# A routed layer of experts on one NeuronCore: the list of next experts placed behind the third slot's gathered tokens, and three closing branches nested

## Chip, core and metric

One core of a Trainium2 chip runs the whole program in one launch. The metric is the device time of one execution in microseconds (us), the median of several runs. The program's instructions lie on five engines, each with its own queue, which wait for one another by semaphores: TensorE (PE; PEld is its weight load), VectorE (DVE), ScalarE (ACT), GpSimd (POOL) and SyncE (SP, here the issuer of plain loads). DMA engines move data between HBM and the on-chip memory; gathers and scatters by a list of indices are issued by GpSimd, large loads by SP.

## The reference

The program computes three stages on 1536 tokens of 512 numbers: a windowed attention with block summaries, a dense layer with ELU, and a layer of 8 experts in which each token goes to one expert. Only the last one matters here:

```python
logits = x @ w_gate
e_idx = np.argmax(logits, axis=1)
probs = softmax(logits)
gate_w = probs[np.arange(N), e_idx]
eom = 1.0 / (1.0 + np.exp(-(x @ w_output_gate)))
for e in range(E):
    mask = e_idx == e
    h = np.maximum(x[mask] @ w1[e], 0.0)
    ye = h @ w2[e]
    out[mask] = gate_w[mask, None] * eom[mask, e, None] * ye
```

An expert's weights are w1 (512x1024) and w2 (1024x512), in float32.

## The kernel before, in words

`part1` computes attention and the dense layer; its last steps already choose two experts from the first 1152 tokens and load the weights of the first of them. `part2` calls `second`, which is the layer of experts, and ends with three branches for rare loads of tokens.

The tokens are sorted into *slots* of 128 that share an expert. Slots 0 and 1 are the early ones; slots 2 to 10 are full slots, the entries 11 and 12 of `SEQ` are pairs of half slots of 64 tokens with an expert each, and entries 13 to 15 are the three conditional ones (`PX`). The order is 0, 1, 2, 3, 4, 11, 5, 6, 12, 7, 8, 9, 10. "The third slot" is number 2. For each slot:

- `x_load` (key `xg`, L1082): GpSimd gathers 128 rows of 2 KB from `mdram`; the gather of the slot two places on is issued behind the transposes of this one.
- `x_T` (key `xT`, L1096): TensorE transposes them in four matmuls into one PSUM bank (`T`, a single one); `x_hi2` (`xh`, L1101, ScalarE) and `x_lo2` (`xl`, L1105, VectorE) write them as a high and a low float32r half, and with the low half the bank is free for the next slot's transposes.
- `mm1` (L1121) and `mm2` (L1164): 24 matmuls each (high by high, low by high, high by low weights). The half slots use plain float32 weights (`mm1_two` L1130, `mm2_two` L1173).
- `evac2` (L1177, ScalarE) scales the result, and `scatter` (L1180, GpSimd) writes it to the output by a list of row numbers.

The weights of the full slots have one place on the chip, `w2s`, with a high and a low half for each of 16 blocks of 128x512 floats, and a raw copy in `wo`. `renew(slot, part)` (key `cv`, branch at L1204, conversions L1189 and L1195) is a branch on ScalarE and VectorE: only where the slot's expert differs from the one before does it convert the raw blocks of this part (8, 4 and 4 blocks). Behind each part `load_next` (key `ld`, L1402 to L1411) makes SP load the blocks of the *next different* expert into `wo`, on the condition that it isn't the one loaded before. Which expert that is stands in `nxi`, the list of next experts; `route_a3` (key `a3`, L948 to L964, eight instructions of VectorE) computes it. `route_a5` (key `a5`, L985 to L1000, eight instructions) computes the experts of the half slots and the number that decides the three closing branches. The half slots' weights come by `w_direct` (L1054): 256 KB a load, 25 of them at once into memory that is free by then (`spare`), the rest as places come free; they are issued behind a5.

The order of all this is written by a small planner in `second`. Each operation is entered with a key, an engine, an estimated duration and the keys it must stand behind (`op(key, engine, duration, deps, function)`); the planner picks, over and over, the operation that can start first by its estimates, and emits it. So `deps` set the place of an instruction in its engine's queue; the waits that the data need are set by the framework from the tiles that are read and written. In the order that results before the change, VectorE does a3 and a5 right behind the lists of tokens (`li`), SP issues the three loads of `ld` 1 and then the 25 direct loads, and the transposes of the fifth slot (`xT` 4) stand on TensorE behind the last matmul of slot 1 and ahead of the first matmul of slot 2.

At the end, each of the three `If` blocks holds the loads, the gather and the whole work of one pair of half slots; with these inputs none is taken. An engine that skips a block still passes a compare-and-branch and instructions that bring the semaphores to where the block would have left them; on GpSimd one of them is INC_SWDGE_SEM (L1425).

Of the kernel before, what the change touches and what calls it, by code (L numbers as in the profile page):

```python
# [67 lines left out]
KF = 11  # L68
PB, PX = 2, 3
# [10 lines left out]
class Prog:  # L80
# [1132 lines left out]
    def second(self, seq, t, start=False):  # L1213

        nc, N, C = self.nc, len(seq), COST
# [9 lines left out]
        def mm(q, key, d, deps, fn, used=()):  # L1225
            pe[q].append((key, d, deps, fn, used))

        def op(key, eng, d, deps, fn):
            fixed.append((key, eng, d, deps, fn))
# [41 lines left out]
        f = [i for i in range(N) if full[i]]  # L1271
        for p, i in zip(f, f[1:]):
            known = [("f", 2)] if i > 1 else []
            op(("cv", i, 0), "Act", C["if"], [("on", "m1", p, 1, 3) if i in (1, 3) else ("gl", p, 1), ("xl", i)] + known, lambda i=i: self.renew(seq[i], 0))
            op(("cv", i, 1), "Act", C["if"], [("on", "m2", p, 3), ("cv", i, 0)] + known, lambda i=i: self.renew(seq[i], 1))
            op(("cv", i, 2), "Act", C["if"], [("on", "m2", p, 7), ("cv", i, 1)] + ([("o", p)] if i > 1 else []) + known, lambda i=i: self.renew(seq[i], 2))
            for part in range(3):
                if seq[i] not in nxt:
                    continue
                op(("ld", i, part), "SP", 0.1, [("cv", i, part), ("a3",)], lambda i=i, part=part: self.load_next(nxt[seq[i]], PARTS[part]))  # L1280

        half, at = [], {}
        if start:
            J = NBLK - 1
            for i in range(TPB[J]):
                e, d = ("DVE", C["l"]) if i == 1 else ("Act", C["a"])
                mm("c", ("yl", i), C["m"], [], lambda i=i: self.mm_y1(J, NF - 1, i))
                op(("m", i), e, d, [("yl", i)], lambda i=i: self.out_y1(J, i))
                op(("md", i), "Pool", C["g"], [("m", i)], lambda i=i: self.store_m(nc.gpsimd, J, i))
            for i in range(TPB[J]):  # L1290
                e, d = ("DVE", C["l"]) if i == 1 else ("Act", C["a"])
                mm("c", ("lt", i), C["t"], [("m", i)], lambda i=i: self.lg_turn(J, i))
                op(("mt", i), e, d, [("lt", i)], lambda i=i: self.lg_parts(J, i))
            for i in range(TPB[J]):
                mm("c", ("lg", i), 0.84, [("mt", i)], lambda i=i: self.lg2(J, i))
            op(("lv",), "DVE", 0.12, [("lg", i) for i in range(TPB[J])], self.lg3)
            op(("rb",), "DVE", 1.62, [("lv",)], lambda: self.route_block(J))
            mm("c", ("cnt",), 0.05, [("rb",)], self.count)
            mm("c", ("rm",), 0.05, [("rb",)], lambda: self.rank_mm(TE, NTT, self.fin))
            op(("left",), "DVE", 0.1, [("cnt",)], self.left)  # L1300
            op(("ga",), "DVE", 0.3, [("rb",)], lambda: self.route_gate_a(J))
            op(("ge",), "Act", 0.25, [("ga",)], lambda: self.route_gate_e(J))
            op(("a2",), "DVE", 2.75, [("left",)], self.route_a2)
            op(("rk",), "DVE", 0.35, [("rm",)], lambda: self.rank_of(TE, NTT, self.fin))
            op(("gb",), "DVE", 0.6, [("ge",)], lambda: self.route_gate_b(J))
            op(("gc",), "Pool", 1.4, [("gb",)], lambda: self.route_gate_c(J))
            op(("a4",), "DVE", 1.05, [("a2",)], self.route_a4)
            op(("b1",), "DVE", 2.3, [("a4",), ("rk",)], self.route_b)
            op(("pp",), "Pool", 0.58 * (NTT - PD), [("b1",)], lambda: self.places(nc.gpsimd, PD, NTT))
            op(("pv",), "DVE", 0.2 * PD, [("b1",)], lambda: self.places(nc.vector, 0, PD))  # L1310
            op(("b2",), "DVE", 1.45, [("b1",), ("gc",)], self.route_w)
            mm("c", ("inv",), 0.4, [("b2",), ("pp",), ("pv",)], lambda: self.invert(self.slots_of(), NTT))
            op(("li",), "DVE", 1.4, [("inv",)], lambda: setattr(self, "L_", self.lists("L", self.slots_of(), NL)))
            for i in (2, 3):
                op(("xg", i), "Pool", C["g"], [("li",)], lambda i=i: self.x_load(seq[i]))
            op(("f", 2), "Act", 0.46, [("li",)], lambda: self.flag(2))
            op(("a3",), "DVE", 1.6, [("li",)], self.route_a3)
            op(("a5",), "DVE", 1.75, [("li",)], self.route_a5)
            for i in range(2):
                done["xl", i] = 0.0  # L1320

            for i in range(16):
                if i < WN:
                    done["w", chain[0], i] = 0.0
                    continue
                self.ew[0, i] = self.new_place(f"wi{i}")
                op(("h0", i), "Act", C["hAct"], [], lambda i=i: self.conv_hi("Act", 0, i, self.ew[0, i]))
                op(("w", 0, i), "DVE", C["l"], [("h0", i)], lambda i=i: self.last_w(i))
        else:
            done["xg", 0] = C["xg"]  # L1330
            for i in range(16):
                done["w", chain[0], i] = C["xg"]
            half = [(0.0, p) for i in range(8) for p in self.float_places(f"wi{i}")]
# [15 lines left out]
        while any(pe.values()) or fixed:  # L1349
# [20 lines left out]
            st, _, d, kind, o, eng = best  # L1370
            t[eng] = end = st + d
            if kind == "pe":
                q, o = o
# [39 lines left out]
    def part2(self):  # L1413
        nc, tc = self.nc, self.tc
        J = NBLK - 1
        self.split_g(J, NF - 1)
        self.mm_y(J, NF - 2)
        for k, s in enumerate(range(KF + PB + PX)):
            self.par[s] = k % 2
        self.flag(0)  # L1420
        self.flag(1)
        self.second((0, 1) + SEQ, START2, True)
        n = nc.values_load(self.esi[0:1, LF + NY:], min_val=0, max_val=4 * NL, skip_runtime_bounds_check_because="a sum of counts of slots")  # L1423
        for s in range(KF + PB, KF + PB + PX):
            with tc.If(n > 2 * (s - 2)):  # L1425
                w = self.sets(s)[0]
                for i in range(16):
                    self.w_direct(w, i, self.rw[i])
                self.x_load(s)
                self.second((s,), dict(PE=0, Act=0, DVE=0, Pool=0))  # L1430
# [63 lines left out]
```

## Time and profile before

| | us |
|---|---|
| median of three runs | 575.3 |
| lowest and highest of them | 572.5, 576.26 |
| the profiled execution | 575.26 |
| its span, first to last instruction | 573.1 |
| TensorE's mean granted clock, share of full speed | 0.968 |

Times in the profile count from the start of the span. A row of a timeline has the start, the duration, the engine, the line, the operation, what it writes and reads, how often, and in brackets the idle time before it with what ended it. Engines with a q (DVEq, POOLq, SPq) are their queues: branches, semaphores, DMA issues. PEclk is the granted clock of TensorE, 1.00 for 2.4 GHz and 0.50 for 1.2 GHz.

### The profile page before, as it was taken

The numbers are of one execution on the slowest core, as the hardware profiler recorded it, in microseconds if no ns is written. First come the engines' busy times: TensorE is split into PE (matmuls) and PEld (weight loads), VectorE is DVE, ScalarE is ACT, GpSimd is POOL, SyncE is SP. The second block draws the span as 40 slices with busy tenths as digits, with TensorE's granted clock in tenths as the row PEclk, the third lists the DMA queues.
The fourth block names the chain that finished last, engine by engine and source line by source line (L and its number), as shares of the span: only waits on it lengthen the run. The fifth ranks groups of instructions, "written<-read, shape, count | busy, mean of one in ns | idle before, by whom it ended". The sixth has DMA issues, their size and how long they took to land. (4 is left out here: it accounts for less than half of the span.)

```text
span 573.1 us, 9644 instructions
## 1 busy us (share of the span) xinstructions
PE 533.8 (93%) x3089; PEld 425.1 (74%) x3089; DVE 375.6 (66%) x978; ACT 317.1 (55%) x774; POOL 137.2 (24%) x180
## 2 busy tenths in 40 slices
PE   7877997899869999999999999999979999999994
PEld 4466675577658888988888888978858665675883
DVE  6999999999967886786665778986711100444510
ACT  5774666656557876775665756762213222555620
POOL 3556245326970000000000001421412111100001
PEclk8979999899889999999999999998989999999998
DMA  9999743241223220311000003331299486494601
GB/s 283 293 342 403 221 157 119 87 131 59 68 79 121 61 79 15 116 47 46 17 1 28 28 1 123 120 108 38 70 389 387 144 317 210 156 363 147 238 29 39
DMA packets 39003, 81.34 MB, mean 142 GB/s; under 512 B 4127, under 2 KB 9631, under 8 KB 38944
## 3 DMA queue, kind: packets, MB, share of 16 engines
q1 hardware_dynamic: 36624, 73.30, 38.5%
q0 software_dynamic: 2320, 7.34, 3.6%
q8 instruction: 26, 0.43, 0.3%
q14 instruction: 33, 0.27, 0.2%
HBM read 103.70 MB, written 6.55 MB: 192 GB/s over the span
## 5 line engine op out<-in xcount | busy, mean ns | idle before, releaser
L422 PE MATMUL h<-xh,wi 128*128 128x384 f32 (+2 forms) x528 | 144.3, 341 | 2.4 <-ACT wi L152 1.8
L465 PE MATMUL y<-wsp,gh 128*128 128x512 f32 x368 | 117.3, 407 | 5.4 <-DVE wsp L176 5.0
L422 PEld LDWEIGHTS h<-xh,wi 128*128 128x128 f32 x528 | 94.8, 192 | 10.5 <-ACT wi L152 2.3
L422 PE MATMUL h<-xl,wi 128*128 128x384 f32 (+2 forms) x264 | 88.8, 336 | 0.0
L465 PEld LDWEIGHTS y<-wsp,gh 128*128 128x128 f32 x368 | 67.3, 191 | 19.7 <-DVE wsp L176 6.9
L465 PE MATMUL y<-wsp,gl 128*128 128x512 f32 x184 | 70.5, 403 | 0.0
L1153 DVE TENSOR_TENSOR holdl<-S,holdh 128x512 fp32r<-128x512 f32 x22 | 15.2, 690 | 80.9 <-ACT holdh L1149 53.7
L1121 PE MATMUL h<-w2s,holdh 128*128 128x512 f32 x176 | 62.0, 413 | 0.0
L1164 PE MATMUL y<-w2s,holdh 128*128 128x512 f32 x176 | 59.1, 398 | 0.0
L422 PEld LDWEIGHTS h<-xl,wi 128*128 128x128 f32 x264 | 50.5, 191 | 3.8 <-issue 0.2
L176 DVE TENSOR_TENSOR wsp<-wo,wsp 128x512 fp32r<-128x512 f32 x62 | 47.6, 769 | 8.1 <-ACT wsp L175 7.5
L175 ACT CAST wsp<-wo 128x512 fp32r<-128x512 f32 x62 | 38.2, 619 | 21.7 <-PE y L465 14.5
L434 DVE SCALAR_TENSOR_TENSOR elt<-ele,elt 128x384 f32<-128x384 f32 (+2 forms) x64 | 38.8, 606 | 16.9 <-ACT ele L432 16.5
L445 ACT CAST gh<-elp 128x384 fp32r<-128x384 f32 (+2 forms) x62 | 31.5, 508 | 30.1 <-DVE elp L435 21.9
L431 ACT ACTIVATE elt<-h 128x384 f32<-128x384 f32 (+2 forms) x64 | 31.3, 490 | 24.1 <-PE h L422 19.9
L435 DVE SCALAR_TENSOR_TENSOR elp<-elt,elp 128x384 f32<-128x384 f32 (+2 forms) x64 | 41.9, 654 | 3.5
L446 DVE TENSOR_TENSOR gl<-elp,gh 128x384 fp32r<-128x384 f32 (+2 forms) x62 | 37.3, 602 | 7.6 <-ACT gh L445 6.5
L1121 PEld LDWEIGHTS h<-w2s,holdh 128*128 128x128 f32 x176 | 34.5, 196 | 8.5 <-ACT w2s L1189 0.8
L465 PEld LDWEIGHTS y<-wsp,gl 128*128 128x128 f32 x184 | 35.0, 192 | 7.5 <-DVE gl L446 0.3
L1164 PEld LDWEIGHTS y<-w2s,holdh 128*128 128x128 f32 x176 | 33.1, 188 | 8.4 <-issue 1.6
L336 ACT ACTIVATE e<-e,nb 128x120 f32<-128x120 f32 x88 | 33.7, 388 | 9.3 <-DVE nb L324 9.2
L1121 PE MATMUL h<-w2s,holdl 128*128 128x512 f32 x88 | 35.4, 402 | 0.0
(290 smaller groups left out, 951.0 us busy)
## 6 DMA issues: line engine op xcount, KB each, us to landing
wo<-in_w SPq DMA_DIRECT2D x9, 2048.0 KB
wo<-in_w SPq DMA_DIRECT2D x18, 1024.0 KB
ri<-in_w_in SPq DMA_DIRECT2D x16, 512.0 KB
ro<-in_w_out SPq DMA_DIRECT2D x16, 512.0 KB
wo<-in_w SPq DMA_DIRECT2D x32, 256.0 KB
w2p<-in_w SPq DMA_DIRECT2D x32, 256.0 KB
w2q<-in_w SPq DMA_DIRECT2D x24, 256.0 KB
q<-in_q SPq DMA_DIRECT2D x18, 256.0 KB
```

Of the source, the lines that this page charges most:

```text
L175: nc.scalar.copy(w[:, 0], f)
L176: nc.vector.tensor_tensor(w[:, 1], f, w[:, 0].bitcast(F32), op=ALU.subtract)
L336: nc.scalar.activation(e[:, p], e[:, p], AF.Exp, bias=nb[:, p:p + 1], scale=0.125, accum_out=sm[:, p:p + 1])
L422: nc.tensor.matmul(h, lhsT=w[:, wl, k * 128:k * 128 + 128], rhs=x[:, k, a:b], start=(n == 0), stop=(n == 11))
L431: nc.scalar.activation(t, h, AF.Tanh, scale=0.5)
L434: nc.vector.scalar_tensor_tensor(t, e, 1.0, t, op0=ALU.add, op1=ALU.mult)
L435: nc.vector.scalar_tensor_tensor(p, t, 0.0, p, op0=ALU.min, op1=ALU.add)
L445: nc.scalar.copy(gh, p)
L446: nc.vector.tensor_tensor(gl, p, gh.bitcast(F32), op=ALU.subtract)
L465: nc.tensor.matmul(self.y[j][t], lhsT=gx[:, sl], rhs=wx, start=(c == 0 and n == 0), stop=(c == NF - 1 and n == len(ops) - 1))
L1121: nc.tensor.matmul(self.h[s, hf], lhsT=x[:, k], rhs=w, start=(n == 0), stop=(n == 11))
L1164: nc.tensor.matmul(self.y2[s], lhsT=g[:, ks], rhs=w, start=(i == 0 and n == 0), stop=(i == 7 and n == 2))
```

## The change

The conversions of a slot (`cv`) get one more key to stand behind: the load of their own part, `("ld", p, part)`, for every slot behind the second. a3 stands behind `("xl", 2)`, the third slot's low half, instead of `("li",)`; a5 behind a3 and the second part of the third slot's `renew`. And the three closing `If` blocks are entered one within the other: each begins inside the body of the one before, and all end together.

```diff
--- before.py
+++ after.py
@@ -1271,9 +1271,10 @@
         f = [i for i in range(N) if full[i]]
         for p, i in zip(f, f[1:]):
             known = [("f", 2)] if i > 1 else []
-            op(("cv", i, 0), "Act", C["if"], [("on", "m1", p, 1, 3) if i in (1, 3) else ("gl", p, 1), ("xl", i)] + known, lambda i=i: self.renew(seq[i], 0))
-            op(("cv", i, 1), "Act", C["if"], [("on", "m2", p, 3), ("cv", i, 0)] + known, lambda i=i: self.renew(seq[i], 1))
-            op(("cv", i, 2), "Act", C["if"], [("on", "m2", p, 7), ("cv", i, 1)] + ([("o", p)] if i > 1 else []) + known, lambda i=i: self.renew(seq[i], 2))
+            raw = lambda part: [("ld", p, part)] if i > 1 else []
+            op(("cv", i, 0), "Act", C["if"], [("on", "m1", p, 1, 3) if i in (1, 3) else ("gl", p, 1), ("xl", i)] + known + raw(0), lambda i=i: self.renew(seq[i], 0))
+            op(("cv", i, 1), "Act", C["if"], [("on", "m2", p, 3), ("cv", i, 0)] + known + raw(1), lambda i=i: self.renew(seq[i], 1))
+            op(("cv", i, 2), "Act", C["if"], [("on", "m2", p, 7), ("cv", i, 1)] + ([("o", p)] if i > 1 else []) + known + raw(2), lambda i=i: self.renew(seq[i], 2))
             for part in range(3):
                 if seq[i] not in nxt:
                     continue
@@ -1314,8 +1315,8 @@
             for i in (2, 3):
                 op(("xg", i), "Pool", C["g"], [("li",)], lambda i=i: self.x_load(seq[i]))
             op(("f", 2), "Act", 0.46, [("li",)], lambda: self.flag(2))
-            op(("a3",), "DVE", 1.6, [("li",)], self.route_a3)
-            op(("a5",), "DVE", 1.75, [("li",)], self.route_a5)
+            op(("a3",), "DVE", 1.6, [("xl", 2)], self.route_a3)
+            op(("a5",), "DVE", 1.75, [("a3",), ("cv", 2, 1)], self.route_a5)
             for i in range(2):
                 done["xl", i] = 0.0
 
@@ -1421,8 +1422,9 @@
         self.flag(1)
         self.second((0, 1) + SEQ, START2, True)
         n = nc.values_load(self.esi[0:1, LF + NY:], min_val=0, max_val=4 * NL, skip_runtime_bounds_check_because="a sum of counts of slots")
-        for s in range(KF + PB, KF + PB + PX):
-            with tc.If(n > 2 * (s - 2)):
+        with ExitStack() as ctx:
+            for s in range(KF + PB, KF + PB + PX):
+                ctx.enter_context(tc.If(n > 2 * (s - 2)))
                 w = self.sets(s)[0]
                 for i in range(16):
                     self.w_direct(w, i, self.rw[i])
```

## Rows read from the trace of the kernel before

**Rows 1.** Page: busy us of each engine, share of the span, instructions.
```profile
PE 533.8 (93%) x3089; PEld 425.1 (74%) x3089; DVE 375.6 (66%) x978; ACT 317.1 (55%) x774; POOL 137.2 (24%) x180
```

**Rows 2.** Busy time by stretch: stretch, us, busy by engine, PEclk, DMA share, GB/s.
```profile
414.00:416.00 2.00, 2.00 (x12) 1.68 (x11) 0.69 (x1) 0.59 (x1) 0.94 (x1) 1.00 0.86 269
...
418.00:420.00 2.00, 0.00 (x0) 0.00 (x0) 0.00 (x0) 0.00 (x0) 0.00 (x0) 1.00 1.04 411
...
422.00:424.00 2.00, 2.00 (x6) 1.61 (x5) 0.00 (x0) 0.00 (x0) 1.65 (x2) 0.50 1.05 390
```

**Rows 3.** Timeline of TensorE, 400 to 432: start, us, instruction [idle before, releaser].
```profile
414.06 0.60 PE L1096 MATMUL T<-c,xg 128*128 128x128 f32 x4
...
416.12 0.39 PE L1164 MATMUL y<-w2s,holdl 128*128 128x512 f32 x1
...
416.35 0.40 PE L1164 MATMUL y<-w2s,holdh 128*128 128x512 f32 x1
...
420.69 1.09 PE L1096 MATMUL T<-c,xg 128*128 128x128 f32 x4 [3.94 <-DMA xg<-mdram,gixL]
...
424.34 0.39 PE L1121 MATMUL h<-w2s,holdl 128*128 128x512 f32 x1
```

**Rows 4.** Timeline of VectorE around the list of next experts.
```profile
408.59 0.26 DVE L953 TENSOR_SCALAR f_e<-f_en 128x8 f32<-128x8 f32 x1
...
410.54 0.17 DVE L964 TENSOR_SCALAR nxi<-nxi 128x9 int32<-128x9 int32 x1
...
412.80 0.69 DVE L1105 TENSOR_TENSOR holdl<-T,holdh 128x512 fp32r<-128x512 f32 x1
...
415.31 0.69 DVE L1105 TENSOR_TENSOR holdl<-T,holdh 128x512 fp32r<-128x512 f32 x1 [1.82 <-ACT holdh L1101]
```

**Rows 5.** Timeline of SP's DMA issues, 340 to 428.
```profile
411.73 3.34 SPq L1411 DMA_DIRECT2D wo<-in_w  x3
...
415.89 10.25 SPq L1054 DMA_DIRECT2D w2q<-in_w  x7
```

**Rows 6.** Timeline of GpSimd: gathers (L1082) and a scatter (L1180).
```profile
407.80 1.07 POOL L1082 DMA_INDIRECT xg<-mdram,gixL  x1 [4.08 <-PE y L1164]
...
411.35 1.01 POOL L1180 DMA_INDIRECT out<-o,sixE  x1 [1.22 <-DMA xg<-mdram,gixL]
...
412.66 0.97 POOL L1082 DMA_INDIRECT xg<-mdram,gixL  x1 [0.30 <-PE y L1164]
...
414.93 0.94 POOL L1082 DMA_INDIRECT xg<-mdram,gixL  x1 [1.29 <-PE T L1096]
```

**Rows 7.** DMA issues, median us to landing: 407.5 to 410; 411 to 412; 412.5 to 413.7.
```profile
xg<-mdram,gixL POOLq DMA_INDIRECT x2, 3.4
...
out<-o,sixE POOLq DMA_INDIRECT x1, 6.8
...
xg<-mdram,gixL POOLq DMA_INDIRECT x1, 7.9
```

**Rows 8.** Timeline of ScalarE: the first conversion after 390.
```profile
492.77 4.26 ACT L1189 CAST w2s<-wo 128x512 fp32r<-128x512 f32 x8
```

**Rows 9.** Timeline of TensorE: first matmuls of a pair of half slots.
```profile
454.33 3.65 PE L1130 MATMUL h<-w2q,xt 128*64 128x512 f32 x16
```

**Rows 10.** The tail: last scatter, its landing, queue instructions (ns min/median/max, first to last start).
```profile
566.39 0.98 POOL L1180 DMA_INDIRECT out<-o,sixL  x1 [4.46 <-ACTq L1425]
...
out<-o,sixL POOLq DMA_INDIRECT x1, 3.7
...
L1425 POOLq INC_SWDGE_SEM  x3: 737/748/779, 567.0 to 569.0; - x3
...
L1486 POOLq DRAIN  x1: 2447/2447/2447, 569.8 to 569.8; - x1
...
L1486 SPq DRAIN  x2: 7/7/7, 570.8 to 570.9; - x2
```

**Rows 11.** Queue instructions of `renew`'s branch on VectorE, 412 to 414.5.
```profile
L1204 DVEq EVENT_SEMAPHORE  x1: 21/21/21, 413.5 to 413.5; - x1
```

## The prediction, made before the changed kernel ran

> **What bounds the kernel now.** I read the page's busy times first, then busy time by stretch, then the timelines of the engines around the few places where TensorE rests. TensorE is busy for 93% of the span [rows 1]. In the second layer it works without a break to its last matmul, but for one stretch: from 416 to 424 us it does nothing for four microseconds and then runs at the lower clock (granted share 0.50, which is 1.2 of 2.4 GHz), while the DMA engines move about 390 GB/s [rows 2]. The timeline names the releaser: the transposes of gathered tokens wait 3.94 us for a gather [rows 3]. So time saved at this place moves everything behind it; elsewhere in the layer TensorE itself is the limit. The second place is the tail behind the last matmul, where the other engines end the program.
>
> **What the stall costs.** The last matmul before it starts at 416.35; the next could start 0.23 later (416.12 to 416.35), at 416.58; the transposes start at 420.69. That is 4.11 us. Behind it the clock is down: from the start of the four transposes to the eighth matmul after them it takes 420.69 to 424.34 = 3.65 us, and the same sequence at full clock 414.06 to 416.12 = 2.06. The clock costs 1.59. Together 5.70 us [rows 3].
>
> **Why the gather is late.** VectorE needs 408.59 to 410.71 (2.12 us, eight instructions) for a3, the list of next experts [rows 4]. One microsecond later, at 411.73, SP issues the three loads of the next expert (16 blocks of 128x512 floats, 4.19 MB), and from 415.89 the first of 25 direct loads of 0.262 MB [rows 5]; data flow from about 414 (269 GB/s from 414 to 416) [rows 2]. GpSimd issues the gathers of the third and fourth slot at 407.80 and 1.4 us later, the scatter of the first slot at 411.35, the gather of the fifth slot at 412.66 and the next at 414.93 [rows 6]. The first two landed in 3.4 us each, ahead of the loads; the scatter took 6.8, the fifth slot's gather 7.9 [rows 7]: it landed at 420.6, and the waiting transposes are its own.
>
> **The change, part by part.**
> *a3 behind the third slot's tokens.* Their low half (L1105) runs from 412.80 to 413.49 [rows 4]; a3 follows it in VectorE's order, 413.5 to 415.6. SP's load of the register and the first issue come 1.0 later, as before: 416.6 instead of 411.73, 4.9 us later. The gather of 412.66 then has only the scatter and the next gather beside it. I take 3.4 us, the nearest row (two gathers 1.4 us apart): it lands at 416.1, before 416.58. Bounds: 3.4, and the 6.8 of the scatter under load, which would land it at 419.5. The stall goes, and with it the drop of the clock: 5.7 us.
> *What is late next.* The fourth slot's low half waits behind a3: it starts at 415.6 instead of 415.31 and ends at 416.3; it frees the PSUM bank for the fifth slot's transposes. That is 0.3 before TensorE gets there: it costs nothing, at worst 0.5 if a3 runs longer in its new place.
> *The loads behind a3.* The three loads come 4.9 us later. Their first use is the conversion for the next expert at 492.77 [rows 8]; no earlier slot converts. Nothing.
> *a5 and the direct loads.* a5 (eight instructions, estimated at a3's 2 us) comes behind the fourth slot's low half and two branches of `renew`: 416.5 to 418.7. On SP the direct loads come behind it and behind the three conditional loads of the slot after (same expert, skipped). They start near 419.5, 3.6 us later, while the 4.19 MB still flow (10.8 us at 390 GB/s): DMA has no gap, and the whole train is 4.9 us later. Its first 16 direct loads feed the first pair of half slots, which TensorE reaches at 454.33, and the second eight of them behind 457.98 [rows 9]; 5.7 earlier that is 448.6 and 452.3. Train: 4.19 + 16 x 0.262 = 8.4 MB at 390 GB/s = 21.5 us from about 414, so 435.5; plus 4.9 gives 440.4, and with up to 8 for landing 448.4 for the last of them. Hidden, by 4 us at the tightest.
> *Gathers after it.* The later ones run inside the train, as before, and take 6 to 8 us; each is used about a slot's time after its issue (48 matmuls of 0.23 = 11 us). Nothing.
> *("ld", p, part) as a condition of the conversions.* It keeps the planner from placing a conversion ahead of the load that fills its source; the order of the others stays. Nothing.
> *Three branches nested.* The last scatter is issued at 566.39 and lands 3.7 later, at 570.1; SP is through at 570.9. GpSimd takes three rounds of branch and INC_SWDGE_SEM (0.74 to 0.78 us each), the last from 569.0 to 569.75, then a DRAIN of 2.45 from 569.8 to 572.25, and only then does the closing barrier run [rows 10]. The rounds are (569.0 - 567.0) / 2 = 1.0 apart. Nested, the outer branch skips all three: one round, the drain from 567.8 to 570.25, and SP's 570.9 is last. Gain 572.25 - 570.9 = 1.4. Bounds: 0, if the skipping path still counts for three or the drain waits for something that began with the scatter; no more than 1.4, since the landing stays. On the other side one more increment, 0.8, for a nest's longer skip. I take 1.4, since the drain starts 0.05 after the third increment and nothing else of GpSimd ends near its end.
>
> **Sum.** The profiled execution took 575.26 us for a span of 573.1; the median of the runs is 575.3, so the two may be read as one. 575.26 - 5.7 - 1.4 = 568.2 us.
>
> **The rivals.**
> *The tail keeps its length.* Only 5.7 goes: 569.6. For it: the drain of 2.45 is seen once and what it waits for isn't.
> *The gather is late in part.* The scatter, the next gather and the first loads still overlap it: it lands at 418 to 419, the stall is 1.5 to 2.5, the clock falls or not: 570 to 572. Against: both gathers that had no loads beside them took 3.4.
> *The gather is late for its own reason.* The scatter of 411.35 and the gathers of 412.66 and 414.93 share GpSimd's queue and hold one another up; the loads only add the time of one more quarter of a megabyte, 0.67 us at 390 GB/s. Then it lands at 419.9 instead of 420.6 and the clock falls as before: 575.3 - 0.7 - 1.4 = 573.2. For it: the three are close together. Against: the pair of 3.4 was as close. The Trainium skill (DMA: Bandwidth & Descriptors, Queues, rings and completion order) says that each DMA engine takes turns between the queues that have work, a packet at a time. By that rule a gather beside a stream of loads gets every other turn and loses about its own transfer time, which is this rival; the trace's 7.9 against 3.4 looks unlike such turns, but it doesn't show a gather beside loads alone.
> *The branch waits for its load (slower).* `renew` of the third slot reads what the three loads write. If its wait stood ahead of the branch instead of within it, ScalarE and VectorE would stand there until the loads landed: 416.6 + 2.3 until data flow + 10.8 = 429.7. TensorE's first matmul of the slot would go from 421.4 to there: 575.3 + 8.3 - 1.4 = 582. Against: before, the same branch stands behind the same loads in the order, and VectorE's semaphore behind it came at 413.5 [rows 11], with the loads hardly begun. It decides as soon as the loads land later than 416.6, so at once if it exists.
> *The change does nothing*, the loads coming on by another instruction than a3: 574. The order in the code leaves little room for it.
>
> **How the numbers follow.** Forecast, 568.2: 0.50. Tail unchanged, 569.6: 0.22. Gather late in part, 570 to 572: 0.13. Gather late for its own reason, or nothing done, 573 to 574: 0.09. Slower, 582: 0.04; other losses 0.02. Differences of less than 1% (5.75 us) can't be told from no change here, so 569.5 is the limit: the forecast lies beyond it by 1.3, the case without the tail on it. Faster by over 1%: 0.50 and half of 0.22, so 0.61; slower: 0.04 and half of 0.02, so 0.05; within 1%: the rest, 0.34. The range: 565.8 (the runs of before span 3.8 us, and a quick one may be met) to 571.8.
>
> **What would show it.** Right: no wait of TensorE for a gather near 416 and a granted clock of 1.00 there; the first load near 416.6; the fifth slot's gather landing in under 4 us; the last matmul 5.7 us earlier; one INC_SWDGE_SEM at the end, and the barrier right behind SP's drain. Wrong: a gather of over 5 us with no load in flight; a wait of the half slots for their weights near 448; a DRAIN that ends more than 1 us behind SP's.

## The result, and the profile after

| | before | after |
|---|---|---|
| median of four runs, us | 575.26 | 567.67 |
| lowest and highest | 572.5, 576.26 | 566.79, 567.87 |
| the profiled execution | 575.26 | 567.62 |
| its span | 573.1 | 565.4 |
| TensorE's mean granted clock | 0.968 | 0.977 |

The ratio of the times is 0.9876 with a 95% interval of 0.9853 to 0.9898; the plain quotient of the two medians, 0.9868, lies inside it. The forecast was 568.2.

The page's busy times of after, as in [rows 1]: TensorE has the same 3089 instructions and 2.5 us less busy time; 1.59 of it is the lower clock behind the stall (below), the rest is not traced to a place.

```profile
PE 531.3 (94%) x3089; PEld 422.0 (75%) x3089; DVE 375.8 (66%) x978; ACT 317.3 (56%) x774; POOL 137.0 (24%) x180
```

TensorE at the place of the stall, in the timeline of after, as in [rows 3]:

```profile
413.94 0.60 PE L1096 MATMUL T<-c,xg 128*128 128x128 f32 x4
...
416.01 0.39 PE L1164 MATMUL y<-w2s,holdl 128*128 128x512 f32 x1
416.24 0.39 PE L1164 MATMUL y<-w2s,holdh 128*128 128x512 f32 x1
416.47 0.60 PE L1096 MATMUL T<-c,xg 128*128 128x128 f32 x4
...
418.53 0.39 PE L1121 MATMUL h<-w2s,holdl 128*128 128x512 f32 x1
...
419.89 0.39 PE L1121 MATMUL h<-w2s,holdl 128*128 128x512 f32 x1
```

The bracket with the wait is gone: the transposes at 416.47 follow the last matmul of the slot without a pause. From their start to the eighth matmul behind them it takes 418.53 - 416.47 = 2.06 us, the value at full clock in [rows 3], where it was 3.65. The eighth matmul comes 424.34 - 418.53 = 5.81 earlier; 0.11 of this is older than the stall (416.35 against 416.24 for the matmul ahead of it), so the stall and its clock gave back 5.70. From 394 us to the end of TensorE's work no wait of it is left in the view of waits.

Busy time by stretch in after (as in [rows 2]: stretch, us, busy time and count of PE, PEld, DVE, ACT and POOL, PEclk, DMA share, GB/s); the last three rows are a stretch that the prediction didn't read:

```profile
414.00:416.00 2.00, 2.00 (x12) 1.69 (x11) 1.72 (x7) 0.59 (x1) 0.94 (x1) 1.00 0.47 131
...
422.00:424.00 2.00, 2.00 (x10) 1.62 (x9) 1.02 (x2) 1.19 (x3) 0.00 (x0) 1.00 0.99 351
...
432.00:434.00 2.00, 2.00 (x11) 1.65 (x10) 0.69 (x1) 0.59 (x1) 0.90 (x1) 1.00 0.34 125
434.00:436.00 2.00, 2.00 (x10) 1.65 (x10) 0.00 (x0) 0.00 (x0) 0.00 (x0) 1.00 0.28 102
436.00:438.00 2.00, 2.00 (x11) 1.65 (x10) 0.00 (x0) 0.69 (x1) 0.68 (x1) 1.00 0.52 146
```

The granted clock is 1.00 in all of them. The DMA engines move 131 GB/s in the stretch from 414 to 416, where before it was 269 and rising: 131 GB/s over 2 us is 0.26 MB, the size of one gather, which has them nearly to itself. And between 432 and 438 there is a hole in the stream of loads, of which more below.

VectorE in after, as in [rows 4]:

```profile
412.66 0.69 DVE L1105 TENSOR_TENSOR holdl<-T,holdh 128x512 fp32r<-128x512 f32 x1 [4.24 <-ACT holdh L1101]
413.26 0.24 DVE L953 TENSOR_SCALAR f_e<-f_en 128x8 f32<-128x8 f32 x1
...
415.13 0.17 DVE L964 TENSOR_SCALAR nxi<-nxi 128x9 int32<-128x9 int32 x1
415.22 0.68 DVE L1105 TENSOR_TENSOR holdl<-T,holdh 128x512 fp32r<-128x512 f32 x1
417.09 0.33 DVE L990 TENSOR_TENSOR mask<-rc,f_T 128x160 f32<-128x160 f32 x1 [1.19 <-DVEq L1204]
```

The list of next experts (413.26 to 415.30) now stands between two low halves, and the second of them starts at once at 415.22 and ends at 415.90, 0.6 us before TensorE needs the bank. The first instruction shown of a5 comes at 417.09.

SP's DMA issues in after, as in [rows 5]: the first row is three issues of the big loads and three skipped ones.

```profile
416.33 18.16 SPq L1412 DMA_DIRECT2D wo<-in_w  x6
435.30 4.70 SPq L1054 DMA_DIRECT2D w2q<-in_w  x8
440.20 8.92 SPq L1054 DMA_DIRECT2D w2p<-in_w  x13
```

The first big load goes out at 416.33 instead of 411.73. The direct loads begin at 435.30 instead of 415.89; what SP stood for shows in its queue's waits from 415 to 436 (us in total, times, longest):

```profile
SPq L1412 <- DMA wo<-in_w: 13.1, 3, 8.2
```

The first pair of half slots, as in [rows 9], is nevertheless reached 5.86 us earlier (448.47), and the matmuls of its last four loads follow at the distance of before:

```profile
448.47 3.65 PE L1130 MATMUL h<-w2q,xt 128*64 128x512 f32 x16
...
454.36 1.94 PE L1130 MATMUL h<-w2p,xt 128*64 128x512 f32 x8
```

When the direct loads were in can be counted. The queue of SP's loads moves nothing but them from 436 us on, and its 25 loads are 3600 packets by 458, so 144 each. This is its row in the DMA view of 436 to 450 us (packets, MB, share of 16 engines):

```profile
q1 hardware_dynamic: 2304, 4.20, 86.1%
```

2304 packets are 16 loads: the sixteen that this pair needs first were in at about 450.0.

The tail in after, as in [rows 10], from four views: the last scatter, its landing, the increment, the drains.

```profile
560.53 0.98 POOL L1180 DMA_INDIRECT out<-o,sixL  x1 [4.46 <-ACTq L1425]
```

```profile
out<-o,sixL POOLq DMA_INDIRECT x1, 2.7
```

```profile
L1425 POOLq INC_SWDGE_SEM  x1: 795/795/795, 561.3 to 561.3; - x1
...
L1488 POOLq DRAIN  x1: 2447/2447/2447, 562.1 to 562.1; - x1
...
L1488 SPq DRAIN  x2: 7/7/7, 564.0 to 564.1; - x2
```

One increment instead of three. The scatter landed in 2.7 us instead of 3.7, and the DRAIN of 2.447 begins at 562.1 and ends at 564.5, still 0.5 behind SP's. From the start of the scatter to the end of the span: 573.1 - 566.39 = 6.71 before, 565.4 - 560.53 = 4.87 after.

The account closes: the last matmul starts 5.86 us earlier (5.70 of the stall and 0.16 of small shifts), as does the scatter, and the tail is 1.84 shorter: 7.70, the difference of the two spans.

### The profile page after: what moved, and what is told of

Same layout as the page of the kernel before. It is cut to its first block, busy times and chain, and to the rows that moved or that the text cites. A ratio compares the mean times of both kernels' runs of the same rounds, so it can differ in the third digit from the quotient of the medians.

```text
span 565.4 us, 9609 instructions
## 1 busy us (share of the span) xinstructions
PE 531.3 (94%) x3089; PEld 422.0 (75%) x3089; DVE 375.8 (66%) x978; ACT 317.3 (56%) x774; POOL 137.0 (24%) x180
## 5 line engine op out<-in xcount | busy, mean ns | idle before, releaser
L465 PE MATMUL y<-wsp,gh 128*128 128x512 f32 x368 | 116.0, 403 | 6.1 <-DVE wsp L176 5.9
```

The source lines that it names most:

```text
L465: nc.tensor.matmul(self.y[j][t], lhsT=gx[:, sl], rhs=wx, start=(c == 0 and n == 0), stop=(c == NF - 1 and n == len(ops) - 1))
```

## Experiments

**The two halves apart.** First the kernel before with the three blocks nested and nothing else (e1_nest_only):

```diff
-        for s in range(KF + PB, KF + PB + PX):
-            with tc.If(n > 2 * (s - 2)):
+        with ExitStack() as ctx:
+            for s in range(KF + PB, KF + PB + PX):
+                ctx.enter_context(tc.If(n > 2 * (s - 2)))
```

> The kernel before with the three closing branches nested and nothing else. If the tail is set by GpSimd's rounds of branch and INC_SWDGE_SEM with a drain of fixed length behind them: one INC_SWDGE_SEM, the drain starts 1.6 us behind the start of the last scatter instead of 3.4, and the span ends 4.9 us behind it instead of 6.7; 573.5 us against 575.3, TensorE's wait of 4 us for the gather unchanged. Rival, the shorter tail of the changed kernel comes from a scatter that landed sooner, or from less traffic: 575.3.

Measured: 573.77 us against 574.83 (a quotient of 0.9982), ratio 0.9971 (0.9953 to 0.9990). Its increments in the tail, and TensorE at the stall:

```profile
L1424 POOLq INC_SWDGE_SEM  x1: 795/795/795, 565.9 to 565.9; - x1
```

```profile
419.19 1.09 PE L1096 MATMUL T<-c,xg 128*128 128x128 f32 x4 [3.20 <-DMA xg<-mdram,gixL]
...
422.79 0.39 PE L1121 MATMUL h<-w2s,holdl 128*128 128x512 f32 x1
```

One increment, and a tail of 570.0 - 565.10 = 4.90 us from the scatter to the end; the stall (3.20 in this execution, with a gather of 7.2 us) and the low clock (422.79 - 419.19 = 3.60) are still there. So the nesting acts on the tail and not on the stall. The scatter itself starts later here, 1.32 us behind the start of ScalarE's last scaling (563.78) instead of 566.39 - 565.43 = 0.96: counted from that scaling the end comes 1.45 us sooner than before, not 1.81. Why the scatter starts later isn't shown; in after it starts 0.96 behind.

Then the kernel after with the three blocks one behind another (e2_order_only):

```diff
-        with ExitStack() as ctx:
-            for s in range(KF + PB, KF + PB + PX):
-                ctx.enter_context(tc.If(n > 2 * (s - 2)))
+        for s in range(KF + PB, KF + PB + PX):
+            with tc.If(n > 2 * (s - 2)):
```

> The changed kernel with the three branches one behind the other again. If the two parts add up: no wait of TensorE for the gather, granted clock 1.00 from 396 on, three INC_SWDGE_SEM and a tail of 6.7 us; 569.5 us, 5.8 below before. Rival, that the order alone gives less because the tail absorbs some of it: 571 or more.

Measured: 568.81, ratio 0.9886 (0.9843 to 0.9929). The transposes, the landing of their gather (median us from issue), and the increments:

```profile
415.50 0.60 PE L1096 MATMUL T<-c,xg 128*128 128x128 f32 x4
```

```profile
xg<-mdram,gixL POOLq DMA_INDIRECT x1, 3.3
```

```profile
L1426 POOLq INC_SWDGE_SEM  x3: 737/748/779, 560.1 to 562.2; - x3
```

No wait, a gather of 3.3 us, and a tail of 6.63 with three increments. The two ratios multiply to 0.9857, beside 0.9876 for the whole change: within their intervals the halves add up.

**Which of the two moves frees the gather.** Both from e2_order_only: a5 back at the lists of tokens (e3_a3_only), so that the direct loads go first, and a3 back there (e4_a5_only), so that the big loads do.

```diff
-            op(("a5",), "DVE", 1.75, [("a3",), ("cv", 2, 1)], self.route_a5)
+            op(("a5",), "DVE", 1.75, [("li",)], self.route_a5)
```

> Branches not nested; a3 behind the third slot's tokens as in the change, but a5 right behind the lists as before, so that the 25 direct loads of 256 KB go out first and the three big loads behind them. If any stream of loads delays the gather: it lands after 6 us or more, TensorE waits 2 to 4 us for it near 417, 573 to 576 us. Rival, only the three big loads (2, 1 and 1 MB in one DMA each) delay it: no wait, 569.5.

```diff
-            op(("a3",), "DVE", 1.6, [("xl", 2)], self.route_a3)
+            op(("a3",), "DVE", 1.6, [("li",)], self.route_a3)
```

> Branches not nested; a3 right behind the lists as before, so that the three big loads go out early, and a5 with the direct loads late as in the change. If the big loads alone fill the DMA engines while the gather is in flight: it lands after 7 to 8 us, TensorE waits 3 to 4 us and its clock falls, 574 to 576 us. Rival, it takes the direct loads behind them too: the gather lands in 4 to 5 us and the wait is under 1.5 us, 570 to 571.

e3_a3_only: 572.49, ratio 0.9957 (0.9933 to 0.9982). Its SP issues, its transposes, its gather:

```profile
409.14 5.30 SPq L1054 DMA_DIRECT2D w2q<-in_w  x8
...
429.69 3.85 SPq L1412 DMA_DIRECT2D wo<-in_w  x3
```

```profile
416.59 0.63 PE L1096 MATMUL T<-c,xg 128*128 128x128 f32 x4 [1.96 <-DMA xg<-mdram,gixL]
...
418.66 0.39 PE L1121 MATMUL h<-w2s,holdl 128*128 128x512 f32 x1
```

```profile
xg<-mdram,gixL POOLq DMA_INDIRECT x1, 5.9
```

The direct loads of 256 KB, now first at 409.14, delay the gather too, but to 5.9 us and not to 7 or 8; time and wait come out just below what was expected for a delay by any stream of loads (573 to 576, 2 to 4). The clock did not fall behind the wait: 418.66 - 416.59 = 2.07. This profile is of the quickest of its ten runs (569.45), and 1.0 us of that lies ahead of the stall (the transposes before it start at 411.94, in e2_order_only at 412.97). The median is 3.68 above e2_order_only's, more than this wait: in slower runs it may have been longer, or the clock may have fallen, which no trace shows.

e4_a5_only: 574.59, ratio 1.0000 (0.9976 to 1.0024):

```profile
417.81 1.09 PE L1096 MATMUL T<-c,xg 128*128 128x128 f32 x4 [3.88 <-DMA xg<-mdram,gixL]
...
421.69 0.63 PE L1121 MATMUL h<-w2s,holdl 128*128 128x512 f32 x1
...
423.98 0.39 PE L1121 MATMUL h<-w2s,holdl 128*128 128x512 f32 x1
```

```profile
xg<-mdram,gixL POOLq DMA_INDIRECT x1, 7.8
```

With the big loads early the gather takes 7.8 us, the wait is 3.88 and the clock falls (421.69 - 417.81 = 3.88 for the same sequence). Here it stays down longer: the eighth matmul still takes 0.63. To the fourteenth, which is quick again, it takes 423.98 - 417.81 = 6.17 us, in after 419.89 - 416.47 = 3.42, so the clock costs 2.75. Moving a5 alone brings nothing, moving a3 alone less than half: to lose the whole wait the gather must have no loads beside it, and the change has to hold back both trains.

**The scatter as a cause.** The scatter that GpSimd issues just ahead of the gather is put behind it, in the kernel before (e8_scatter_behind, run once):

```diff
-            op(("s", i), "Pool", C["g"], [("o", i)], lambda: self.scatter(s))
+            op(("s", i), "Pool", C["g"], [("o", i)] + ([("xg", 5)] if start and i == 0 else []), lambda: self.scatter(s))
```

> The kernel before, but GpSimd's scatter of the first slot stands behind the gathers of the fifth and sixth entry instead of ahead of them. If the loads alone delay the gather: it still takes 7 us or more from its start, TensorE's wait 3 to 4 us. Rival, the scatter ahead in GpSimd's queue takes its part: the gather takes 5 to 6 us, the wait is 1 to 2.5 us.

574.05, beside 573.92 for the kernel before on the same chip:

```profile
419.43 0.87 PE L1096 MATMUL T<-c,xg 128*128 128x128 f32 x4 [3.08 <-DMA xg<-mdram,gixL]
...
423.08 0.41 PE L1121 MATMUL h<-w2s,holdl 128*128 128x512 f32 x1
```

```profile
xg<-mdram,gixL POOLq DMA_INDIRECT x1, 7.3
```

The gather without the scatter in front still takes 7.3 us beside the loads, 0.6 less than the 7.9 of [rows 7] but no less than the 7.2 of e1_nest_only, where the scatter is ahead of it; and the stall stays. With e2_order_only, where the scatter is in front and the loads aren't there (3.3), this leaves the loads as the cause.

**The size of the loads.** In the kernel before, the first and largest of the three loads, 2 MB, goes as eight loads of one block each, and the two of 1 MB as four each: 16 loads of 256 KB (e7_small_loads).

```diff
+        if n == 2:
+            for j in which:
+                w = self.a["w1" if j < 8 else "w2"][bass.ds(ev, 1), j % 8].rearrange("o p n -> (o p) n")
+                self.nc.sync.dma_start(self.wo[:, j], w, cond=self.cond[n])
+            return
```

> The kernel before, but the big loads of the next expert go out as 16 DMAs of 256 KB instead of three of 2, 1 and 1 MB, in the same place and with the same bytes. If the size of the DMAs decides how long a gather beside them takes (it took 8.0 us from its start to TensorE's transposes beside the big loads, 6.0 beside direct loads of 256 KB): 6 us, TensorE's wait 2 us and no fall of its clock, 571.5. Rival, the bytes in flight decide: 8 us, a wait of 4 us, 575.

570.82, ratio 0.9952 (0.9935 to 0.9968):

```profile
410.13 12.24 SPq L1413 DMA_DIRECT2D wo<-in_w  x16
```

```profile
416.73 0.63 PE L1096 MATMUL T<-c,xg 128*128 128x128 f32 x4 [1.42 <-DMA xg<-mdram,gixL]
...
418.80 0.39 PE L1121 MATMUL h<-w2s,holdl 128*128 128x512 f32 x1
```

```profile
xg<-mdram,gixL POOLq DMA_INDIRECT x1, 5.4
```

The same bytes, begun 1.1 us ahead of the gather (410.13 and 411.23; 0.9 in [rows 5] and [rows 6]), and the gather takes 5.4 us, the wait is 1.42 and the clock stays (418.80 - 416.73 = 2.07). Against e8_scatter_behind on the same chip the wait is 3.08 - 1.42 = 1.66 shorter and the clock gives back 3.65 - 2.07 = 1.58: together 3.24, near the 3.10 by which the median fell against before. (The two profiled spans differ by 4.4, but 1.03 of that lies ahead of the stall: the transposes before it start at 412.62 and 413.65.) What isn't told apart: SP needs 12.24 us to issue 16 loads and 3.34 for the three [rows 5], so small loads are also fewer bytes queued at once. Either the size of a load or the bytes in the queues sets the delay; no run here separates them.

**The late direct loads.** In the kernel after, the skipped loads of the slot after are put further back in SP's order, so that the direct loads come before them (e5_direct_first):

```diff
-                op(("ld", i, part), "SP", 0.1, [("cv", i, part), ("a3",)], lambda i=i, part=part: self.load_next(nxt[seq[i]], PARTS[part]))
+                op(("ld", i, part), "SP", 0.1, [("cv", i, part), ("a3",)] + ([("m1", 2, 0, 3)] if i == 2 else []), lambda i=i, part=part: self.load_next(nxt[seq[i]], PARTS[part]))
```

> The changed kernel, but SP has the third slot's three conditional loads (skipped, same expert) behind the direct loads instead of ahead of them. In the changed kernel SP stood at them until the big loads had landed, and the direct loads began at 435.3; here they should begin near 419.5, the DMA engines should have no gap between 430 and 440, and the weight loads of the first half slots should name no DMA as releaser. If the late direct loads were hidden to the last: the same time as the changed kernel, 567.7 within 0.6. Rival, they cost TensorE something: 567.0 or less.

568.29, ratio 0.9877 (0.9858 to 0.9896), as good as the change's 0.9876. Its SP issues, and two of the stretches where after has its hole:

```profile
416.98 2.16 SPq L1412 DMA_DIRECT2D wo<-in_w  x3
420.30 14.12 SPq L1054 DMA_DIRECT2D w2q<-in_w  x8
```

```profile
432.00:434.00 2.00, 2.00 (x14) 1.74 (x13) 0.58 (x1) 0.59 (x1) 0.94 (x1) 1.00 1.04 382
434.00:436.00 2.00, 2.00 (x10) 1.67 (x9) 0.11 (x1) 0.00 (x0) 0.00 (x0) 1.00 1.06 388
```

The direct loads go out at 420.30, about where the prediction had them, and the DMA engines run through at 382 to 388 GB/s. So the skipped loads were what held SP, and the delay cost nothing that can be measured. It is 15 us for the first direct load, but only some 5 for the sixteenth, the last that the first pair needs: here SP issues its loads more slowly (434.76 + 7 x 0.79 = 440.3, against 445.0 in after). One part of the expectation failed: the weight loads of the first pair still name a DMA as releaser in three of their gaps. These gaps are 0.29 us, as long as those that name none, and TensorE has no wait there, so they cost nothing either.

**The tail.** The kernel after without the three closing blocks (e6_no_branches), which shows what is left when no round of GpSimd stands there:

```diff
-        with ExitStack() as ctx:
-            for s in range(KF + PB, KF + PB + PX):
-                ctx.enter_context(tc.If(n > 2 * (s - 2)))
...
-                self.second((s,), dict(PE=0, Act=0, DVE=0, Pool=0))
```

> The changed kernel without the three closing conditional blocks (none is taken with these inputs; for others their tokens would be left out). If GpSimd's drain is of fixed length and starts when its queue comes to it: no INC_SWDGE_SEM, the drain starts 1.0 us behind the start of the last scatter instead of 1.6, SP's wait for the landing is then the last, and the span ends 0.5 us sooner behind the scatter: 567.1. Rival, the drain waits for something that began with the scatter: the same end, 567.7.

567.27, ratio 0.9861 (0.9842 to 0.9880), and a tail of 4.75 us:

```profile
L1481 POOLq DRAIN  x1: 4117/4117/4117, 560.7 to 560.7; - x1
```

The last round would be worth 0.12 us of tail, little more than the 0.1 to which spans are given. The time lies between the two that were expected (567.1 and 567.7) and can't tell them apart; the DRAIN can. It begins earlier and lasts longer, 4.117 instead of 2.447, and ends 564.8 - 560.85 = 4.0 behind the start of the last scatter; in after it is 564.55 - 560.53 = 4.0. So it isn't of fixed length, and without a round its end follows something that began with the scatter, as the rival had it. With one round it could be either: the DRAIN starts where the increment ends (561.3 + 0.795 = 562.1) and lasts 2.447, as it does behind two and three, and so ends where the scatter alone would have put it.

Two blocks nested and the third behind them (e9_two_rounds, run once):

```diff
+        for group in ((KF + PB, KF + PB + 1), (KF + PB + 2,)):
+            with ExitStack() as ctx:
+                for s in group:
+                    ctx.enter_context(tc.If(n > 2 * (s - 2)))
```

> The changed kernel with two of the closing branches nested and the third behind them, so that GpSimd passes two rounds of branch and INC_SWDGE_SEM. If every round holds the end up by its own 1.0 us and slows the last scatter: the scatter lands 3 us or more behind its start instead of 2.7, and the span ends 5.8 us behind it (4.9 with one round, 6.7 with three). Rival, a second round still hides behind the landing and the drain: 5.0.

567.05 in its one run, and a tail of 5.81, as expected if every round holds the end up:

```profile
L1426 POOLq INC_SWDGE_SEM  x2: 738/766/793, 559.9 to 560.9; - x2
...
L1489 POOLq DRAIN  x1: 2447/2447/2447, 561.7 to 561.7; - x1
```

| rounds | kernel | end of span | start of last scatter | tail, us | landing of the last scatter, us |
|---|---|---|---|---|---|
| 0 | e6_no_branches | 565.6 | 560.85 | 4.75 | 2.7 |
| 1 | the change | 565.4 | 560.53 | 4.87 | 2.7 |
| 1 | e1_nest_only | 570.0 | 565.10 | 4.90 | 2.7 |
| 2 | e9_two_rounds | 565.0 | 559.19 | 5.81 | 2.9 |
| 3 | e2_order_only | 566.2 | 559.57 | 6.63 | 3.2 |
| 3 | before | 573.1 | 566.39 | 6.71 | 3.7 |

Each round beyond the first costs 0.9 of tail. The rounds also go with a later landing of the scatter: 2.7 with one or none, 2.9 with two (3 or more was expected), and 3.2 to 3.8 with three (3.4 in e3_a3_only and 3.8 in e4_a5_only).

## Why the prediction was right, point by point

*What the stall costs*: 5.70 forecast, 5.70 found, idle time and clock both.

*a3 behind the third slot's tokens*: right in each step. a3 was put at 413.5 to 415.6 and ran from 413.26 to 415.30; the first load was put at 416.6 and went out at 416.33. The gather's landing was taken as 3.4; e2_order_only shows 3.3 for it, and in after the transposes did not wait.

*What is late next*: nothing was, as forecast; the low half was to end 0.3 before TensorE came for the bank and ended 0.6 before.

*The loads behind a3* and *the gathers after it*: nothing, as forecast, since TensorE has no further wait. One gather, that of 417.34, took 8.5 us, above the 6 to 8 that were forecast; its transposes come only at 431.09.

*a5 and the direct loads*: this is the step that failed. "They start near 419.5" and "DMA has no gap": they started at 435.3, with a gap of some 6 us. The prediction counted the three skipped conditional loads ahead of them as free. SP stood at them for 13.1 us, until the earlier loads into the same place had landed: a skipped load waits here as one that is taken. The forecast's "hidden, by 4 us at the tightest" held all the same, by other numbers than its own. It had the sixteenth load in by 448.4, before the second eight are needed; it was in at about 450.0, and they are needed from 451.95 (the first matmul with a load of the second eight). So 2 us were left instead of 4. The matmuls of the sixteenth load itself are the last two of the row at 454.36, at about 455.7, some 6 us behind its landing. That was cover enough, by e5_direct_first, which takes the delay away and gains nothing. But nothing in the forecast limited SP's wait: that it was short enough to hide was luck.

*Three branches nested*: the mechanism was right, the size too small. 1.4 was forecast as the most, "since the landing stays"; it was 1.84. The landing didn't stay: it went from 3.7 to 2.7 with two rounds fewer, and SP's last drain came 564.1 - 560.53 = 3.6 behind the start of the scatter instead of 570.9 - 566.39 = 4.5. GpSimd's drain ended about where it was put, 4.0 behind the scatter's start instead of the forecast 570.25 - 566.39 = 3.9, and is still last, by 0.5 us. So the mis-sized part is SP's end, 570.9, which the forecast took as fixed and as the bound of the gain: it moved with the landing, and the full two rounds of 0.92 came off the tail.

*The conditions ("ld", p, part) of the conversions* were left in all runs from after and not tried alone; that they cost nothing rests on the account above, which closes without them.

The sum, 568.2, is 0.58 above the profiled execution's 567.62: 0.44 of it is the tail, the rest the 0.16 of small shifts. Both are below what the runs of one kernel differ by.

Of the rivals, the unchanged tail and the partly late gather fell with the rows of after, as did the branch that waits for its load and the change that does nothing: behind 416.47 TensorE has no wait. The gather "late for its own reason" fell with e2_order_only and e8_scatter_behind: without loads it takes 3.3 us, with loads and no scatter ahead 7.3. The Trainium skill (DMA: Bandwidth & Descriptors, Queues, rings and completion order) has each DMA engine take turns by packets; the estimate drawn from it, that a gather loses about its own transfer time of 0.67 us, is not what was measured: the loss was 7.8 - 3.3 = 4.5 beside the big loads (e4_a5_only) and 5.4 - 3.3 = 2.1 beside 256 KB ones (e7_small_loads). Whether the rule or the estimate's equal turns fail here isn't shown.

## What to carry to other kernels

Where TensorE waits for a small gather while a large prefetch is on its way, look first at who releases the prefetch: if its data are needed much later, the instruction that frees it can stand behind the gather's last use, and every train of loads has to be held back, since one alone is enough to delay the gather. Count a skipped conditional load as a wait for whatever was last loaded into its place, unless a trace shows otherwise, and look for what is queued behind it. Closing branches that are rarely taken can be put in one nest where each is taken only if the one before it is, so that skipping them costs one round at the end; taking the last round away too was worth no more than 0.1 us here.

## What was unexpected of the hardware

- The delay of a gather of 256 KB depends on the loads beside it: 3.3 us without (e2_order_only), 5.4 and 5.9 beside loads of 256 KB (e7_small_loads, e3_a3_only), 7.2 to 7.9 beside those of 2 and 1 MB (e1_nest_only, e8_scatter_behind, e4_a5_only, before). Whether their size or the bytes queued at once does it stays open.
- Waits of TensorE of 1.42 and 1.96 us (e7_small_loads, e3_a3_only) left its granted clock at 1.00 and cost only themselves; those of 3.08 to 3.94 were followed by the lower clock, 0.50, which cost 1.5 to 1.6 us more behind 3.08, 3.20 and 3.94 (e8_scatter_behind, e1_nest_only, before) and 2.75 behind 3.88 (e4_a5_only). So the cost doesn't go by the length of the wait alone.
- Three loads whose condition is false held SP until the earlier loads into their place had landed, 13.1 us in all. Whether the DMA itself waits or only the semaphore waits that the program has ahead of it isn't shown.
- Rounds of branch and INC_SWDGE_SEM on GpSimd go with a later landing of a scatter that is under way, 2.7 us with one or none, 2.9 with two, 3.2 to 3.8 with three. Why they do isn't shown.
- The DRAIN that closes GpSimd's queue took 2.447 us behind one, two or three rounds and 4.117 with none (e6_no_branches), where it ended 4.0 us behind the start of the last scatter.
